# A weight ring of four places instead of five, one more weight pair resident, and the streamed pairs spread anew

## The chip, the core and the metric

The kernel runs on one core of one Trainium2 chip, which it has to itself. The metric is the device time of one execution in microseconds. A kernel's time is the median of several executions. Where one execution was profiled, its own time stands beside the span of its instructions.

## The reference

The reference returns two independent results side by side, `out[0, :, 0:1024]` and `out[0, :, 1024:2048]`, for a sequence of 2048 rows of 1024 channels in bf16.

Part A is a gated long convolution. `k` is run through a causal filter of four taps and multiplied by `v`; the product is convolved along the sequence with `ssm_k` by FFT (length 4096), a skip term with `ssm_D` is added, and all is multiplied by `q`.

Part B is what matters here, a recurrence over 64 segments:

```python
mem = mem0                                   # [1, 8, 1024]
for s in range(64):
    h = concatenate([mem, x[:, 32*s:32*s+32]], axis=1)   # 40 rows
    q, k, v = (einsum('btd,dhe->bhte', h, W) for W in (Wq, Wk, Wv))   # 32 heads of 128
    scores = where(mask, q @ k.T * 128**-0.5, -1e9)
    o = einsum('bhte,hed->btd', softmax(scores) @ v, Wo)
    mem = o[:, :8]                           # goes into the next segment
    outs.append(o[:, 8:])
```

The memory rows of a segment's output are the memory of the next segment, so the 64 steps cannot run side by side. Each step uses the whole of four weight matrices of 1024 x 4096 bf16, 8 MB each and 32 MB together.

## The kernel before

**Stages.** Part A runs first, in three passes, and beside it TensorE already computes what of part B does not depend on the recurrence (the class `Rows`, line 131: the projections of the last eight rows of each segment, kept in DRAM as `QKBd` and `VBd`). Then comes the loop over 64 segments (lines 908 to 991), and last an output product for eight rows of each segment (lines 996 to 1011). All instructions are written out by hand in their order; nothing is scheduled by a planner.

**Weight pairs.** The weights are handled in 64 pairs of 512 KB, tiles `[128, 2, 1024]`, 4 KB in each of the 128 partitions. Key `("qk", g, i)` is input chunk `i` of Wq and Wk for head group `g` (32 pairs); `("v", g, i)` is chunk `i` of Wv for half `g` of the columns (16 pairs); `("o", g, i)` is two heads of Wo (16 pairs). Below, qk26 is short for `("qk", 2, 6)`, and so on. Lines 58 to 63 sort them into three kinds:

- 45 **resident** pairs lie in on-chip memory for the whole loop.
- 2 **parked** pairs, v01 and qk16, lie in PSUM (line 670), and are copied into a ring place each step by ScalarE and VectorE (`unpark`, lines 716 to 720).
- 17 **streamed** pairs are read from DRAM anew in each step, as listed in `STREAM` (line 40), by group: qk02 qk05, qk13, qk22 qk26, qk32 qk36; v00 v03 v05, v11 v15; o02, o11, o20 o23, o32.

**The ring.** Streamed and unparked pairs live in a pool of `RING = 5` places (line 697). `place()` (line 708) takes the next pair of a fixed list `todo` (the streamed pairs in the order of their use, step after step) and issues one DMA of 512 KB on SyncE's queue (line 713). Ahead of the loop it is called `RING` times (line 901). After that it is called by `done(key)` (line 725), right behind the last matmul that read a streamed or unparked pair: the DMA waits for those matmuls, and then fills the place just freed. For two pairs, qk02 and v03, `done` gives the freed place to a parked pair instead (`PARKED`, line 41). So the load of a pair is issued when the use that lies `RING` uses ahead of it has ended, and every place is at each moment loading, holding a pair that waits, being read, or holding an unparked pair.

**A step on TensorE** (lines 918 to 983), with the ring's uses in brackets: group 0's query and key products [qk02, qk05], half of the v products [v00, v01, v03], group 1's [qk13, qk16], the rest of v's first half [v05], group 2's [qk22, qk26], group 3's [qk32, qk36], the second half of v [v11, v15], then the output product `wo` of groups 0 to 3 [o02; o11; o20, o23; o32]. In between stand the transposes (`tr_a`), scores and the products with V (`pv`) of each group, whose softmax runs on VectorE and ScalarE. At the end `Y_sb` (line 985) and `fill_mem` (line 987) put the new memory rows into `hT`, on which the first product of the next step waits.

A pair of the qk or v kind is four matmuls per 512 columns (`qk_part` line 753, `v_part` line 767), one of the o kind eight of 256 columns (`wo` line 874). The matmuls are the same whether the pair is resident, streamed or parked.

**Other traffic of a step**: `qkb` (128 KB, line 794, SyncE's queue), `H` (line 663, ScalarE's queue), `VB`, `OLd` and four small output DMAs (lines 804, 867, 989, GpSimd's queue).

**Around the loop.** Streamed qk and o pairs are first copied into a contiguous layout `Wst` in DRAM (`relay`, line 122); streamed v pairs are read from `Wv` itself. Resident pairs are loaded beside part A (`open_res`, `res_half`), some of the o kind within step 0 (line 911). In the last step the streamed o pairs are loaded once more, into places of resident pairs that are no longer needed (lines 939 to 943), for the final product.

Of the kernel before, what the change touches and what calls it, by code (L numbers as in the profile page):

```python
# [21 lines left out]
def fused_kernel(ctx: ExitStack, tc, q, k, v, shift_k, ssm_k, ssm_D, outa, x, mem0, Wq, Wk, Wv, Wo, outb, n_seg):  # L22
# [13 lines left out]
    NP = 34  # L36
    NS = 17
    scale = 128.0 ** -0.5
    RING = 5
    STREAM = {"qk": ((2, 5), (3,), (2, 6), (2, 6)), "v": ((0, 3, 5), (1, 5)), "o": ((2,), (1,), (0, 3), (2,))}  # L40
    PARKED = {("qk", 0, 2): ("v", 0, 1), ("v", 0, 3): ("qk", 1, 6)}

    msched = tc.manual_schedule()
# [11 lines left out]
    def keys(m, g, r):  # L55
        return [(m, g, i) for i in r]
# [3 lines left out]
    pairs += [key for g in range(4) for key in keys("o", g, range(4))]  # L60
    streamed = [key for key in pairs if key[2] in STREAM[key[0]][key[1]]]
    parked = list(PARKED.values())
# [42 lines left out]
    def open_res(n):  # L105
        if n:
            pool = cw_.enter_context(tc.tile_pool(name=f"b_wres{len(to_open)}", bufs=1))
            if not wide:
                wide["t"] = pool.tile([128, 8, 2, 1024], BF, name="Wearly")
            for _ in range(n):  # L110
                res_pool[to_open.pop(0)] = pool
# [584 lines left out]
    cp.close()  # L696
    ring = cw_.enter_context(tc.tile_pool(name="b_ring", bufs=RING, reuse_waits="tile"))
    open_res(len(to_open))
# [9 lines left out]
    def place():  # L708

        if todo:  # L710
            key = todo.pop(0)
            t = ring.tile([128, 2, 1024], BF, tag="wring", name="wring")
            nc.sync.dma_start(t[:], Wst[key])
            placed.setdefault(key, []).append(t[:])
# [185 lines left out]

    for _ in range(RING):
        place()
# [113 lines left out]
@with_exitstack  # L1016
def kernel(
    ctx: ExitStack,
    tc: tile.TileContext,
    A_q: bass.AP,  # L1020
    A_k: bass.AP,
    A_v: bass.AP,
    A_shift_k: bass.AP,
    A_ssm_k: bass.AP,
    A_ssm_D: bass.AP,
    B_x: bass.AP,
    B_mem0: bass.AP,
    B_Wq: bass.AP,
    B_Wk: bass.AP,
    B_Wv: bass.AP,  # L1030
    B_Wo: bass.AP,
    B_seg_len,
    out: bass.AP,
):
    assert int(B_seg_len) == 32
    S = B_x.shape[1]
    n_seg = S // 32
    outa = out[0, :, 0:1024]
    outb = out[0, :, 1024:2048]
    with ExitStack() as fctx:  # L1040
        fused_kernel(fctx, tc, A_q[0], A_k[0], A_v[0], A_shift_k, A_ssm_k, A_ssm_D, outa, B_x[0], B_mem0[0],
                     B_Wq.rearrange("d h e -> d (h e)"), B_Wk.rearrange("d h e -> d (h e)"),
                     B_Wv.rearrange("d h e -> d (h e)"), B_Wo.rearrange("h e d -> (h e) d"),
                     outb, n_seg)
# [35 lines left out]
```

## Time and profile before

| | us |
|---|---|
| three executions | 2148.29, 2157.45, 2145.75 |
| median | 2148.29 |
| the profiled execution, its own time | 2154.46 |
| its span, first to last instruction | 2152.6 |
| TensorE, matmul busy | 1720.4 (80% of the span) |
| VectorE busy | 1117.8 (52%) |
| ScalarE busy | 921.1 (43%) |
| GpSimd busy | 419.9 (20%) |
| DMA: bytes moved, mean rate | 728.63 MB, 338 GB/s |
| ring loads: number, size | 1083, 512 KB each |

The profile is one execution. Its page gives busy times of the engines, the chain of work that ended last, and the costliest groups of instructions, one line each: line of the kernel, engine, operation, out<-in by the program's names, number, busy time in us, mean ns of one, and the idle time of the engine just ahead of them with what ended it. A TensorE that waits shows as idle time ahead of a group, put down to what released it; a DMA's time is that from its issue to its landing. The span exceeds the sum of the loop's steps by part A ahead of it and the final product behind it: the step-ending copy of line 894 runs 63 times, from 454.8 to 2059.2 us.

### The profile page before, as it was taken

Reading aid. Unit: us, or ns where it says so; the run is one execution under the profiler, and the core shown is the slowest. Engines: PE = TensorE matmul, PEld = TensorE weight load, DVE = VectorE, ACT = ScalarE, POOL = GpSimd, SP = SyncE. Lnnn points to the kernel's source line nnn. Section 1 sums busy time; section 2 is a strip of 40 time slices with the busy share of each in tenths; the row PEclk is TensorE's granted clock in tenths of the full one; section 3 lists DMA queues with packets and bytes.
Section 4 is the critical chain, followed back from the end, with each engine's and each line's share of the span. In section 5 each row is a group of like instructions: output and inputs, shape, how many; then the busy total and the mean of one; then the engine's idle time right before and its main releaser. Section 6 shows DMA issues by size and latency. Waiting matters only on the chain. (4 is left out here: it accounts for less than half of the span.)

```text
span 2152.6 us, 74044 instructions
## 1 busy us (share of the span) xinstructions
PE 1720.4 (80%) x30514; PEld 895.9 (42%) x30514; DVE 1117.8 (52%) x3364; ACT 921.1 (43%) x2282; POOL 419.9 (20%) x1023
## 2 busy tenths in 40 slices
PE   4788987777887887788788888888888878788879
PEld 2332232334443444444444444444444444444448
DVE  6895842245554555555455555555555545555530
ACT  4546741134444444444444444444444444444430
POOL 4003630011111111111111221111111111221110
PEclk8999999889999999999999999999999999999999
DMA  7798969699999999999999999999999999999990
GB/s 238 287 337 312 360 236 355 215 364 360 364 374 323 363 372 368 354 354 352 337 368 369 373 352 372 369 364 365 361 354 367 363 346 375 366 369 371 367 321 22
DMA packets 267375, 728.63 MB, mean 338 GB/s; under 512 B 64751, under 2 KB 75903, under 8 KB 266525
## 3 DMA queue, kind: packets, MB, share of 16 engines
q1 hardware_dynamic: 241294, 687.24, 86.9%
q0 software_dynamic: 15520, 22.06, 3.3%
q10 hardware_dynamic: 10224, 14.62, 1.9%
q8 instruction: 239, 3.92, 0.7%
q14 instruction: 98, 0.80, 0.1%
HBM read 673.52 MB, written 56.56 MB: 339 GB/s over the span
## 5 line engine op out<-in xcount | busy, mean ns | idle before, releaser
L753 PE MATMUL qkacc<-Wqk,hT 128*32 128x512 bf16 x4096 | 339.5, 384 | 0.0
L753 PEld LDWEIGHTS <-hT 128*32 128x32 bf16 x8192 | 185.9, 96 | 241.9 <-issue 92.1
L874 PEld LDWEIGHTS <-OT 128*32 128x32 bf16 x8192 | 210.2, 96 | 108.9 <-issue 59.2
L874 PE MATMUL yacc<-Wo,OT 128*32 128x256 bf16 x5632 | 237.1, 274 | 16.7 <-ACT OT L863 14.7
L753 PE MATMUL qkacc<-wring,hT 128*32 128x512 bf16 x2048 | 207.5, 394 | 32.8 <-DMA wring<-Wstqk 26.5
L767 PE MATMUL vacc<-wring,hT 128*32 128x512 bf16 x1536 | 143.0, 387 | 100.2 <-DMA wring<-in_B_Wv_dram 98.4
L720 DVE COPY wring<-park 128x1024 bf16<-128x1024 bf16 x128 | 88.6, 692 | 242.3 <-PE vacc L767 164.0
L767 PE MATMUL vacc<-Wv,hT 128*32 128x512 bf16 x2560 | 209.8, 382 | 0.0
L767 PEld LDWEIGHTS <-hT 128*32 128x32 bf16 x4096 | 111.3, 95 | 226.4 <-issue 152.4
L833 ACT ACTIVATE P<-S 128x128 bf16<-128x128 f32 x256 | 71.1, 278 | 314.0 <-DVE S L825 233.5
L789 ACT COPY QK<-tp 128x256 bf16<-128x256 bf16 x256 | 95.4, 373 | 237.2 <-PE tp L780 237.2
L788 POOL COPY QK<-qkb 128x64 bf16<-128x64 bf16 x256 | 61.4, 240 | 652.9 <-PE tp L780 487.3
L753 PE MATMUL qkacc<-Wearly,hT 128*32 128x512 bf16 x2048 | 166.4, 403 | 18.5 <-DVE hT L894 17.9
L852 DVE COPY PB<-P 32x160 bf16<-32x160 bf16 x896 | 173.7, 194 | 10.6
L837 DVE TENSOR_REDUCE sm<-P 128x4 f32<-128x256 bf16 x256 | 107.5, 420 | 130.3 <-ACT P L834 130.3
L719 ACT COPY wring<-park 128x1024 bf16<-128x1024 bf16 x128 | 130.7, 1021 | 103.8 <-PE qkacc L753 100.8
L759 ACT CAST qks<-qkacc 128x512 bf16<-128x512 f32 x256 | 150.8, 589 | 28.8 <-PE qkacc L753 23.3
L874 PE MATMUL yacc<-wring,OT 128*32 128x256 bf16 x2520 | 126.4, 274 | 36.2 <-DMA wring<-Wsto 35.2
L863 ACT CAST OT<-otacc 128x256 bf16<-128x256 f32 x256 | 98.4, 384 | 126.8 <-PE otacc L859 126.8
L989 POOL DMA_DIRECT2D out_dram<-Y_sb x256 | 129.1, 511 | 89.9 <-ACT Y_sb L985 87.9
L824 DVE TENSOR_REDUCE mx<-S 128x4 f32<-128x160 f32 x256 | 83.2, 325 | 107.3 <-PE S L821 102.4
L780 PE MATMUL tp<-ident,qks 128*128 128x128 bf16 x1024 | 102.1, 222 | 42.6 <-ACT qks L759 39.3
(216 smaller groups left out, 2827.1 us busy)
## 6 DMA issues: line engine op xcount, KB each, us to landing
wring<-Wstqk SPq DMA_DIRECT2D x448, 512.0 KB, 6.3
wring<-in_B_Wv_dram SPq DMA_DIRECT2D x320, 512.0 KB, 6.7
wring<-Wsto SPq DMA_DIRECT2D x315, 512.0 KB, 6.0
SK<-s_sb SPq DMA_DIRECT2D x8, 1024.0 KB, 7.0
SU<-s_sb SPq DMA_DIRECT2D x8, 1024.0 KB, 6.7
QKBd<-stq ACTq DMA_DIRECT2D x4, 2048.0 KB, 10.9
Kg<-SK SPq DMA_DIRECT2D x16, 512.0 KB, 6.9
Ug<-SU SPq DMA_DIRECT2D x16, 512.0 KB, 7.5
```

The source lines that it names most:

```text
L719: nc.scalar.copy(t[:, 0, :], park[key][0][:])
L720: nc.vector.tensor_copy(t[:, 1, :], park[key][1][:])
L753: nc.tensor.matmul(u.qk[p0:p0 + 32, :], lhsT=hT[:, kc, :], rhs=w[:, t, c2 * 512:(c2 + 1) * 512], start=(kc == 0), stop=(kc == 7), tile_pos ...
L759: nc.scalar.copy(u.qks[:], u.qk[:])
L767: nc.tensor.matmul(vacc[0][32 * c:32 * c + 32, :].rearrange("p (n x) -> p n x", n=2), lhsT=hT[:, kc, :], rhs=w[:, :, c * 256:(c + 1) * 256 ...
L780: nc.tensor.transpose(tp[:, j * 128:(j + 1) * 128], src[:, j * 128:(j + 1) * 128], ident[:])
L789: nc.scalar.copy(u.QT.rearrange("e (c j) r -> e c j r", c=2), tv[:, 0])
L837: nc.vector.tensor_reduce(out=sm[:], in_=Pv.rearrange("p b x k -> p x b k"), op=ALU.add, axis=AX.XY)
L852: (nc.vector if by[c] == "D" else nc.gpsimd).tensor_copy(to, src)
L863: nc.scalar.copy(u.OT[:].rearrange("e (c i) q -> e i c q", i=2), ov[:, :, :, 0:32])
L874: nc.tensor.matmul(Y[32 * dq:32 * dq + 32, 0:256], lhsT=u.OT[:, hh, 0:32], rhs=w[:, hh % 2, dq * 256:(dq + 1) * 256], start=(u.g == 0 and ...
L989: nc.gpsimd.dma_start(outb[32 * s:32 * s + 24, dq * 256:(dq + 1) * 256], Y_sb[32 * dq + 8:32 * dq + 32, :])
```

## The change

Two constants change; no other line does.

```diff
-    RING = 5
-    STREAM = {"qk": ((2, 5), (3,), (2, 6), (2, 6)), "v": ((0, 3, 5), (1, 5)), "o": ((2,), (1,), (0, 3), (2,))}
+    RING = 4
+    STREAM = {"qk": ((2, 5), (3,), (1, 4, 6), (2, 6)), "v": ((3, 5), (1, 5)), "o": ((2,), (1,), (1,), (2,))}
     PARKED = {("qk", 0, 2): ("v", 0, 1), ("v", 0, 3): ("qk", 1, 6)}
```

The ring has four places of 4 KB per partition instead of five, and the memory of the fifth holds a 46th resident pair. The streamed pairs are 16 instead of 17: v00, qk22, o20 and o23 become resident, and qk21, qk24 and o21, resident before, are streamed. In order of use a step's ring uses are now qk02, qk05, [v01], v03, qk13, [qk16], v05, qk21, qk24, qk26, qk32, qk36, v11, v15, o02, o11, o21, o32, the bracketed ones unparked. The order of the work on TensorE, ScalarE and VectorE stays as it was.

## The prediction

> **What bounds the kernel now.** I read first the share of the DMA engines by stretch, then TensorE's waits, then the times from issue to landing, then the timeline of a step.
>
> The DMA engines' busy tenths in 40 slices, from the page, then one stretch of 400 us (columns: busy us of each engine, granted clock, DMA share, GB/s):
>
> ```profile
> DMA  7798969699999999999999999999999999999990
> ```
>
> ```profile
> 1000.00:1400.00 400.00, 323.12 (x6724) 170.42 (x6723) 205.26 (x701) 175.12 (x476) 77.31 (x219) 0.99 0.98 363
> ```
>
> In the loop the DMA engines are busy 98% of the time, TensorE (first number) 81%. The clock is full, so nothing is lost there.
>
> The copy that ends a step, from the instructions of line 894, and TensorE's waits (us in total, times, longest):
>
> ```profile
> L894 DVE COPY hT<-mt_tp x63: 191/192/193, 454.8 to 2059.2; 128x64 bf16<-128x64 bf16 x63
> ```
>
> ```profile
> PE vacc L767 <- DMA wring<-in_B_Wv_dram: 98.4, 151, 8.6
> ...
> PE yacc L874 <- DMA wring<-Wsto: 35.2, 71, 1.3
> ...
> PE qkacc L753 <- DMA wring<-Wstqk: 26.5, 40, 3.4
> ```
>
> (2059.2 - 454.8) / 62 = **25.88 us a step**. TensorE waits for ring loads 98.4 + 35.2 + 26.5 = 160 us, 2.5 us a step. Without them a step takes 25.88 - 2.5 = 23.4; I use 23.5, because a little of ScalarE's work now hides in those waits. Of this floor 21.1 us is matmuls; the rest is the chains through softmax and the new memory rows, and nothing in the change touches them.
>
> The ring loads, from the DMA list and the ring tile's summary (number, size, median us to landing):
>
> ```profile
> wring<-Wstqk SPq DMA_DIRECT2D x448, 512.0 KB, 6.3
> wring<-in_B_Wv_dram SPq DMA_DIRECT2D x320, 512.0 KB, 6.7
> wring<-Wsto SPq DMA_DIRECT2D x315, 512.0 KB, 6.0
> ```
>
> ```profile
> DMA to landing us min/median/max: 3.2/6.3/9.6
> ```
>
> A load takes 6.35 us on the mean, yet 3.24 us when alone (issued at 394.30, with nothing else under way). The difference is queueing. Going through steps 8 to 57, two landings lie 1.44 us apart; only v05's comes 2.07 and o32's 2.41 after the one ahead, because small transfers (VB and outputs; qkb and H) pass between. The sum is 17 x 1.44 + 0.55 + 0.95 = 25.98, which is the step. So **the step is the DMA engines' time**, and the ring is deep enough to keep them full. It also closes over the places: 17 loads x (6.35 loading + 0.48 waiting landed + 0.5 being read and reissued) + 4.8 for the two unparked pairs = 129.4 = 5 places x 25.9.
>
> **The change, part by part.**
>
> *16 loads instead of 17.* That removes 1.44 us of DMA time a step: 16 x 1.44 + 1.5 = 24.54. SyncE issues 63 DMAs fewer (0.33 us each, its time not on the path). The matmuls are as many and of the same shape.
>
> *Four places.* A load is issued when the use four ahead of it has ended, not five. What the lost place costs depends on the time between those two uses. I took each use's mean start from the trace and removed the waits for loads (us from the step's start): qk02 0.55, qk05 1.31, v01 2.42, v03 3.03, qk13 4.45, qk16 5.43, v05 6.21, [qk21 7.69, qk24 8.63,] qk26 9.06, qk32 11.04, qk36 12.14, v11 13.32, v15 15.55, o02 16.64, o11 18.40, [o21 19.30,] o32 21.86. The bracketed uses are new; I place them from the neighbours, 0.21 us a pair. From a use to the one that it frees the place for:
>
> - before (five on): qk05 to v05 4.90, v00 to qk22 5.70, all others over 6.5;
> - after (four on): **qk16 to qk26 3.63, qk13 to qk24 4.18**, qk21 to qk36 4.45, qk24 to v11 4.69, v05 to qk32 4.83, qk05 to v05 4.90, all others over 5.2.
>
> Such a stretch must hold 0.40 of reading, 0.10 to the issue, the load, and 0.04 to the matmul. The heavy place is group 2, where three streamed pairs now lie in 1.4 us and two of the four places have just held unparked pairs.
>
> *Walk through a step.* Issue = end of the freeing use + 0.10. Landing = the later of issue + L and the last landing + 1.44 (+ 0.55 for v05, + 0.95 for o32). A use starts at landing + 0.04 or in its turn, and a wait shifts all behind it. With five places this gives 25.98 for every L up to 5, against 25.88 measured. With four and L = 4.5: v05 is issued at 1.81, lands at 6.31, wait 0.10. qk24 is issued at 4.95, behind qk13, and lands at 9.45 where its turn is 8.73: wait 0.72. qk26 is issued at 5.97, lands 1.44 behind qk24 at 10.89: wait 1.01. qk16 and v11 wait 0.10 together. Sum 1.93; 23.5 + 1.93 = **25.43**. The waits at v00 and v03 are gone, and group 2 is late in their place; its transposes, scores and softmax stand behind qk26 and shift with it, as TensorE's order has nothing to put ahead of them.
>
> *L, a load's time with little ahead of it*, decides. Rows: 3.24 alone; 15 loads that found under one load's packets not yet started: 3.3 to 6.0, median 4.77; loads with three others under way median 6.0, with four 6.5, but those are queueing and belong to the 1.44. By the walk the step is 24.54 for L up to 3.6 (the DMA bound again), 24.93 at 4.0, 25.43 at 4.5, 25.73 at 4.8, 26.03 at 5.0, 27.03 at 5.5. I take 4.5: nearer to 4.77, since in the loop other traffic runs beside, but under it, since ten of the 15 were v pairs, which meet the most small transfers.
>
> The Trainium skill, "DMA: Bandwidth & Descriptors", section "Anatomy of one DMA", gives a fixed 2.0 us plus bytes at 436 GB/s: an estimate of 3.2 us for 512 KB. The lone load (3.24) agrees; by that rule four places would do, and the step would be 24.54. The same page's section "Latency and other measured facts" speaks against the change: memory latency is 0.2 us on average but 2 us at high load, and the fixed part lightens only with the load. Added to 3.2 that is an estimate of 5.0 us, and the step would be 26.03; the 4.77 of the trace lies between the two.
>
> *The rest.* v00 is loaded into resident memory and not the prologue's small ring, the relays are 12 as before, and step 0 loads one resident o pair more and one streamed pair less: nothing, hidden beside part A, with 3 us either way. The last step reloads four o pairs instead of five, ahead of a transfer on which the final product waits (17 us, in the chain): -1.4.
>
> *Sum.* (25.4 - 25.88) x 63 = -30, and -1.4: -32 on the profiled execution's 2154.5, so 2122. That execution lay 6.2 above the median of 2148.3; in terms of the median **2116 us**.
>
> **The rivals.**
>
> 1. *The saving comes in full.* L stays under 3.6, and the step falls to the DMA bound: (24.54 - 25.88) x 63 - 1.4 = -86, median 2062. For it speaks the 3.24; against it that no loaded stretch shows loads this short but for one of the 15.
> 2. *The ring becomes the bound, and the kernel is slower.* One mechanism: the load for qk24 and qk26, issued behind qk13 and qk16, is not shorter than 5.0 because group 2's three loads, VB and the outputs share the engines there. From L = 4.95 the walk passes 25.9. At 5.5 it is 27.03: +1.15 x 63 - 1.4 = +71, median 2219. For it speak the loaded rows (v05's own median is 5.6) and that over the places 4 x 25.9 leaves only 5.7 us a load for loading and waiting, where now 6.8 are spent; against it that most of the 6.35 is queueing, of which one place less removes up to 1.44.
> 3. *Loss and saving cancel*, L near 4.9, within 0.5% (about what a measurement of this kernel can tell from no change, 11 us).
>
> That the change does not do what it says is no case: the built program has 16 ring loads a step on SyncE's queue.
>
> **How the numbers follow.** Chances: my forecast (step 24.9 to 25.7, median 2085 to 2136) 0.42, full saving 0.18, cancelling 0.13, slower 0.27. So faster 0.60, same 0.13, slower 0.27. The likeliest case gives 2116. The 8 in 10 range cuts a tail of each side: 2055, just under the full saving, to 2195, a step of 26.6, which L = 5.3 gives. The forecast's own range is 2085 to 2136.
>
> **What would show it.** Right: 1020 ring loads; a median to landing near 5.1; TensorE's waits for vacc down by more than half, and waits of qkacc for the ring, at qk24 and qk26, of some 1.7 us a step as the longest of its DMA waits; DMA share a little lower, 0.95 or so; the step-ending copies 25.4 apart. Rival 1 would show 0.98 and 24.5, with waits spread over all pairs; rival 2 landings over 5.3 and waits for Wstqk over 2 us a step. Wrong at the root: a step under 24.5, or waits that do not stand in group 2.

## The result and the profile after

| | before | after |
|---|---|---|
| median of 4 executions, us | 2147.02 | 2235.54 |
| lowest to highest | 2139.11 to 2157.45 | 2227.37 to 2238.7 |
| ratio, 95% interval | | 1.0412 (1.0379 to 1.0445) |
| profiled execution: own time / span | 2154.46 / 2152.6 | 2236.32 / 2234.5 |
| a step of the loop | 25.88 | 27.27 |

The kernel is 4.1% slower, where 1.5% faster was predicted; the time lies above the range of 2055 to 2195. (A fourth execution of before came with this result.) An execution over 1.5% above the fastest of its kernel is left out of the ratios given here and below, in experiment 1 three of four.

Of the 81.9 us by which the span grew, the loop has (2141.7 - 450.7) - (2059.2 - 454.8) = 86.6; the part ahead of it became 4.1 shorter and the tail 0.6.

The step, from the instructions of line 894 after: (2141.7 - 450.7) / 62 = 27.27.

```profile
L894 DVE COPY hT<-mt_tp x63: 190/192/193, 450.7 to 2141.7; 128x64 bf16<-128x64 bf16 x63
```

The DMA engines after, from the page and from the same stretch of 400 us (TensorE's busy us first; at the end of the line granted clock, DMA share, GB/s):

```profile
DMA  7799887899998999999999999999999999999990
```

```profile
1000.00:1400.00 400.00, 311.49 (x6496) 165.88 (x6492) 202.18 (x689) 170.69 (x463) 70.43 (x206) 0.99 0.95 329
```

The tenths look as before, and the share fell only from 0.98 to 0.95. But the engines moved 329 GB/s instead of 363, 9% less. The share alone would hide that.

TensorE's waits for ring loads after (us in total, times, longest):

```profile
PE vacc L767 <- DMA wring<-in_B_Wv_dram: 117.4, 103, 7.4
PE qkacc L753 <- DMA wring<-Wstqk: 101.7, 149, 3.0
PE yacc L874 <- DMA wring<-Wsto: 59.0, 98, 1.8
```

They sum to 278 us, 4.4 a step, against 160 and 2.5. The growth of 1.9 is more than the step's 1.39; the rest was given back where other waits became shorter behind a TensorE that comes later (the transposes' wait for `qks` fell from 39.3 us to 12.9). All three kinds of pair wait longer, the q and k pairs by far the most: nearly four times as long.

The loads after, from the DMA list (median us to landing) and the ring tile's summary:

```profile
wring<-Wstqk SPq DMA_DIRECT2D x512, 512.0 KB, 5.8
wring<-in_B_Wv_dram SPq DMA_DIRECT2D x256, 512.0 KB, 5.7
wring<-Wsto SPq DMA_DIRECT2D x252, 512.0 KB, 5.9
```

```profile
DMA to landing us min/median/max: 3.5/5.8/10.7
```

This is the line that decides. The median went from 6.3 to 5.8, not to the 5.1 that the prediction gave as a sign of being right.

Group 2 of one step after, from the timeline (start, duration; in brackets the idle time ahead and its releaser). The four uses are v05, qk21, qk24 and qk26:

```profile
1166.44 0.40 PE L767 MATMUL vacc<-wring,hT 128*32 128x512 bf16 x4 [1.00 <-DMA wring<-in_B_Wv_dram]
...
1167.90 0.40 PE L753 MATMUL qkacc<-wring,hT 128*32 128x512 bf16 x4
...
1169.17 0.40 PE L753 MATMUL qkacc<-wring,hT 128*32 128x512 bf16 x4 [0.27 <-DMA wring<-Wstqk]
...
1170.58 0.40 PE L753 MATMUL qkacc<-wring,hT 128*32 128x512 bf16 x4 [0.79 <-DMA wring<-Wstqk]
```

v05 comes late, and the three pairs behind it start 1.3 to 1.5 us apart; on the mean of steps 8 to 57 their loads land 1.57, 1.53 and 1.37 us after the load ahead, near the 1.44 of a full queue. On the mean of steps 8 to 59 the waits are v05 1.20, qk21 0.10, qk24 0.49, qk26 0.71, then v11 0.34, o02 0.23, o21 0.49, o32 0.17, and under 0.15 each elsewhere.

### The profile page after: what moved, and what is told of

Same layout as the page of the kernel before. It is cut to its first block, busy times and chain, and to the rows that moved or that the text cites. A ratio compares the mean times of both kernels' runs of the same rounds, so it can differ in the third digit from the quotient of the medians.

```text
span 2234.5 us, 73957 instructions
## 1 busy us (share of the span) xinstructions
PE 1741.9 (78%) x30485; PEld 907.6 (41%) x30514; DVE 1123.8 (50%) x3364; ACT 928.6 (42%) x2282; POOL 416.9 (19%) x1023
## 5 line engine op out<-in xcount | busy, mean ns | idle before, releaser
L753 PEld LDWEIGHTS <-hT 128*32 128x32 bf16 x8192 | 190.5, 97 | 332.1 <-issue 191.4
L753 PE MATMUL qkacc<-wring,hT 128*32 128x512 bf16 x2304 | 238.0, 401 | 108.6 <-DMA wring<-Wstqk 101.7
L874 PE MATMUL yacc<-Wo,OT 128*32 128x256 bf16 x6144 | 251.4, 274 | 18.2 <-ACT OT L863 17.0
L767 PE MATMUL vacc<-Wv,hT 128*32 128x512 bf16 x2816 | 238.6, 388 | 0.0
L767 PE MATMUL vacc<-wring,hT 128*32 128x512 bf16 x1280 | 129.4, 390 | 119.6 <-DMA wring<-in_B_Wv_dram 117.4
L767 PEld LDWEIGHTS <-hT 128*32 128x32 bf16 x4096 | 112.3, 96 | 228.0 <-issue 146.8
L865 DVE CAST OL<-otacc 128x64 bf16<-128x64 f32 x252 | 52.4, 208 | 209.2 <-ACT OT L863 208.5
L874 PE MATMUL yacc<-wring,OT 128*32 128x256 bf16 x2016 | 100.9, 275 | 61.0 <-DMA wring<-Wsto 59.0
```

The lines of the kernel that those rows point to most:

```text
L753: nc.tensor.matmul(u.qk[p0:p0 + 32, :], lhsT=hT[:, kc, :], rhs=w[:, t, c2 * 512:(c2 + 1) * 512], start=(kc == 0), stop=(kc == 7), tile_pos ...
L767: nc.tensor.matmul(vacc[0][32 * c:32 * c + 32, :].rearrange("p (n x) -> p n x", n=2), lhsT=hT[:, kc, :], rhs=w[:, :, c * 256:(c + 1) * 256 ...
L874: nc.tensor.matmul(Y[32 * dq:32 * dq + 32, 0:256], lhsT=u.OT[:, hh, 0:32], rhs=w[:, hh % 2, dq * 256:(dq + 1) * 256], start=(u.g == 0 and ...
```

## The experiments

Two theories were put against each other. **A**: four places are too few for 512 KB loads, because a load hardly gets shorter when one fewer is under way; the new spread is not to blame. **B**: the new spread, with three streamed pairs in group 2, is to blame. Later ones look at why v05 is late although little lies ahead of it. A step is always that between the copies that end a step (line 894, in some kernels a few lines off) in the profiled execution, and a load's time the mean from issue to landing in the loop. The traces tell the landing of 86 to 88% of the loads, and the means are over these.

**1. Before, with four places** (17 loads, the old spread).

```diff
-    RING = 5
+    RING = 4
```

> Four places alone, with the old 17 streamed pairs in their old spread. Theory A (a ring load with little ahead of it takes some 5.4 us in the loop, not 4.5, and the stretch from a use to the fourth after it is too short for that): the walk through a step gives 29.6 us a step at 5.35 us a load, so 2148 + 3.7 x 63 = about 2380 us; at 4.5 us a load it would be 27.0 and 2220. Rival B (the new spread is at fault, three streamed pairs crowded into group 2): the old spread has no such crowd, so the time stays within 30 us of before, under 2180.

Measured: 2429.45 us, the median of four executions between 2388.8 and 2437.2. The profiled one took 2426.7 us at a granted clock of 0.925, the shortest 2388.8 at 0.944. Its step is 30.30 and its load 5.72, against 6.39 with five places. Waits stand at v03 0.74, qk13 1.14, v05 0.84 and o23 1.58: at other pairs than after, since the old spread has other short windows. A part of the 30.30 can be TensorE's lower clock. The shortest execution lies 243 us above before (2145.3), so one place costs some 3.9 us a step by itself, near the 3.7 of A's walk, and B falls.

**2. After, with five places** (16 loads, the new spread). Memory has no room for it, so pair o33 is left out and its products read o31.

```diff
-    RING = 4
+    RING = 5
...
+        key = ("o", 3, 1) if key == ("o", 3, 3) else key
```

> Sixteen loads alone: the new spread with five places. There is no memory for it, so the pair o33 is neither loaded nor kept, and its matmuls read o31 instead (as many matmuls of the same shape). Theory A: the stretches are five uses long again, the walk gives 24.8 us a step at 5.35 us a load, so about 2148 - 66 = 2082 us, DMA busy 0.97 or more. Rival B: group 2 still has its three streamed pairs, TensorE still waits there over 1 us a step, and the time is not under 2140.

Measured: 2061.97 us, ratio 0.9614 (0.9557 to 0.9672); step 24.67, load 6.23. The prediction's bound for 16 loads was 24.54. The stretch and the landings of this kernel:

```profile
1000.00:1400.00 400.00, 335.10 (x7172) 180.72 (x7172) 221.83 (x761) 187.78 (x511) 79.03 (x228) 0.99 0.99 360
```

```profile
DMA to landing us min/median/max: 3.3/6.3/10.6
```

The DMA engines are full again. TensorE's waits for v pairs, which cost 117.4 us after, have almost gone:

```profile
PE qkacc L754 <- DMA wring<-Wstqk: 76.8, 105, 5.1
...
PE vacc L768 <- DMA wring<-in_B_Wv_dram: 17.9, 19, 4.3
PE yacc L875 <- DMA wring<-Wsto: 5.4, 17, 0.9
```

So the streamed pairs of the change are worth what was forecast, and the place costs 27.27 - 24.67 = 2.60 us a step, twice what the load saves (25.88 - 24.67 = 1.21). In the old spread, too, the place costs more than a load saves (experiment 1), so the place is the loss in both.

**3. Before, with four places and one o load fewer** (16 loads in the old windows).

```diff
-    RING = 5
-    ... "o": ((2,), (1,), (0, 3), (2,))}
+    RING = 4
+    ... "o": ((2,), (1,), (0,), (2,))}
```

> Four places and 16 loads as in the changed kernel, but in the old spread with only o23 made resident. Theory A: the tight stretches are now qk05 to qk13 (3.14 us) and v00 to v05 (4.01 us), the walk gives 28.3 us a step at 5.35 us a load, so about 2300 us, slower than the changed kernel, with the waits at qk13 and v05. Rival B (the new spread is at fault): not above 2160.

Measured: 2286.52 us, ratio 1.0649 (1.0580 to 1.0717); step 28.12. A's walk had 28.3. The new spread is 0.85 us a step better than this one, so against the old windows it is a gain, not the loss.

**4. After, without small transfers**: the output stores of all steps but the last, and the VB reloads, are left out.

```diff
-            nc.gpsimd.dma_start(outb[...], Y_sb[...])
-        if not last:
-            load_vb(s + 1)
+            if last:
+                nc.gpsimd.dma_start(outb[...], Y_sb[...])
```

> The changed kernel without the small output stores of line 989 (but for the last step's) and without the reloads of VB after the first; output rows and the products with VB are then not the reference's. Theory A in its general form (any load with little ahead takes 5.4 us): v05 still takes over 5 us, the step stays at about 26.7 to 27.2, the time above 2200 us. Rival C (loads are long because those small transfers run beside them at the start of a step): v05's load falls to 4.5 us or less, the step to about 25.4, the time to 2120 us.

Measured: 2225.53 us, ratio to before 1.0369 (1.0300 to 1.0438), which overlaps that of after; step 26.93, v05's load 5.0 instead of 5.36. The small transfers have about 0.35 us of v05's load and not the main part.

**5. After, with three places.**

```diff
-    RING = 4
+    RING = 3
```

> The changed kernel with three places (the memory of the fourth unused). At most three loads are under way, so little queueing is left and the landing times show what a load takes by itself. Theory A (a floor of 5.0 to 5.4 us in the loop, whatever is under way): median to landing 5.0 or more, the walk gives 33 to 36 us a step, the time 2600 to 2760 us. Rival F (the 5.4 of four places is still queueing, and a load falls towards the lone 3.24 as fewer are under way): median 4 us or less, the step under 29, the time under 2350 us.

Measured: 2615.7 us in one execution, beside 2150.7 for before; step 33.23, load 4.98.

```profile
1000.00:1400.00 400.00, 279.58 (x5227) 142.06 (x5221) 161.45 (x550) 137.62 (x372) 57.75 (x168) 0.91 0.81 264
```

```profile
DMA to landing us min/median/max: 3.1/5.0/9.2
```

The means of qk13 (4.28) and qk21 (4.23) are the lowest here, but they mix two kinds of load. Of the 38 landings of qk13 in steps 8 to 57, 14 took 3.14 to 3.39 us and 23 took 4.63 to 5.39. What tells them apart is the backlog. A load is 128 packets of 4 KB, so one can count how many packets of earlier ring loads have yet to start when a load is issued (steps 1 to 62; median us from issue to landing, and number of loads):

| packets yet to start | 0 | 1 to 63 | 64 to 127 | 128 to 255 |
|---|---|---|---|---|
| three places | 3.21 (17) | 4.47 (138) | 4.88 (310) | 5.27 (403) |
| four places, 17 loads (experiment 1) | 3.27 (15) | 4.48 (42) | 4.94 (121) | 5.78 (628) |

The 14 short loads of qk13 had 0 to 3 packets ahead of them, the 23 long ones 13 to 66. So the 3.24 of the lone load is reached inside the loop, by loads with almost nothing of the ring ahead, and less than half a load ahead already costs over 1 us. Why the step between the two is so large is not shown. The sentence in the expectation of experiment 9 on qk13 and qk21, "a load that found nothing ahead took 4.2 to 4.3 us", does not hold.

**6. After, with the streamed v pairs laid out contiguously too**, like the q, k and o pairs; so far their 4 KB rows are read 8 KB apart from `Wv`.

```diff
-    relaid = [key for key in streamed if key[0] != "v"]
+    relaid = list(streamed)
...
-    for m, g, i in streamed:
-        if m == "v":
-            Wst[m, g, i] = Wv[...]
```

> The changed kernel, with the streamed v pairs also copied once into the contiguous layout ahead of the loop, as the qk and o pairs are, and streamed from there. Rival E (v05 and v15 are long because their 4 KB rows lie 8 KB apart in Wv): their loads fall below 4.8 and 5.4 us, the step by 0.6 us, the time to 2200 us or less. Theory A (any load with little ahead): as the changed kernel, 2225 to 2245 us.

Measured: 2212.84 us, ratio to before 1.0261 (1.0182 to 1.0340), an interval that lies below that of after; step 27.04. v05's load fell from 5.36 to 4.52 and the mean of its packets from 248 to 194 ns (v15's from 217 to 181). The layout is part of v05's lateness, but the step gains only 0.23 of the 0.84 (0.36 by the medians): the time falls between the two expectations. The 8 KB alone cannot be the reason: v03, whose rows lie in the same way, went from 176 to 169 ns only, and in experiment 2 v05's packets took 178 ns without the copy. The copy changes the spacing of the rows and their place in DRAM, and no run parts the two.

**7. After, each ring load as two DMAs of 256 KB.**

```diff
-        nc.sync.dma_start(t[:], Wst[key])
+        for n in range(2):
+            nc.sync.dma_start(t[:, n, :], Wst[key][:, n, :])
```

> The changed kernel, each ring load issued as two DMAs of 256 KB (2 KB a row). Theory A with a floor that is per DMA and not per byte: the halves land as late as the whole, the second 0.3 us later for its issue, the time 2230 to 2280 us. Rival D (the long part of a load is its own bytes on its slowest engine): the halves land in 4.5 us or less and the time falls under 2190 us.

Measured: 2350.8 us in one execution; step 29.07. Half the bytes take 5.1 us at the median, the whole took 5.8:

```profile
DMA to landing us min/median/max: 2.6/5.1/8.6
```

The halves queue beside each other: from the first half's issue to the second's landing 5.83 us pass on the mean, as for the whole load of after. Smaller pieces in the same four places are worse, by more than A had expected, and rival D's fall did not come. Their rows are 2 KB; such packets took 97 ns on the mean, twice 97 against 185 for one of 4 KB. Why the step grew by 1.8 us with a pair landing as soon, this run does not show.

**8. Four places, with the 16 loads spread by the walk of the prediction** (fed with 5.4 us a load).

```diff
-    STREAM = {"qk": ((2, 5), (3,), (1, 4, 6), (2, 6)), "v": ((3, 5), (1, 5)), "o": ((2,), (1,), (1,), (2,))}
+    STREAM = {"qk": ((2, 5), (2,), (3, 4, 7), (2,)), "v": ((3, 6), (0, 2, 6)), "o": ((2,), (0,), (3,), (0,))}
```

> Four places and 16 loads with a spread chosen by the walk at 5.4 us a load among those that the order of the prologue's loads allows: qk02 qk05 v03 qk12 v06 qk23 qk24 qk27 qk32 v10 v12 v16 o02 o10 o23 o30. Theory A: the walk gives 26.2 against 26.8 for the changed kernel, so 40 us faster than it, about 2195 us, and still slower than before (2148). Rival B (another spread would bring the gain of the 16 loads, 2065 to 2090): under 2140 us.

Measured: 2265.82 us, ratio 1.0532 (1.0487 to 1.0576); step 27.72. This expectation failed, the time even has the other sign against after. The walk behind it had left out the small transfers that pass ahead of v06 (0.55 us) and o30 (0.95). With them, reckoned after the run, it gives 27.03 for this spread and 26.83 for the changed one: slower, as measured, but by 0.2 where 0.45 was found. Waits stand at qk24 1.08, qk27 0.68 and o30 1.10. Only three spreads were run with four places, so a better one is not excluded.

**9. After, with two places.**

```diff
-    RING = 4
+    RING = 2
```

> The changed kernel with two places, so that a load finds at most one other under way. With three places a load that found nothing ahead took 4.2 to 4.3 us (qk13, qk21) and one behind another 5.2. Theory A as it stands now (some 4.2 us from issue to landing with nothing ahead, more with a load ahead): median to landing 4.2 to 4.7, the walk gives 42 to 46 us a step, the time 3150 to 3400 us. Rival F (a load alone takes 3.24 as the one lone load of the profile did, all above is queueing): median under 3.7, the step under 38, the time under 2900 us. A floor of 5.0 whatever is ahead would give 48 us and 3540.

Measured: 3278.85 us in one execution, beside 2147.9 for before; step 43.66, load 4.26.

```profile
1000.00:1400.00 400.00, 252.67 (x4034) 121.42 (x4033) 125.81 (x426) 108.95 (x288) 43.03 (x130) 0.80 0.66 203
```

With three of five places gone, a load still takes two thirds of its time with five. Both a floor of 5.0 and rival F fall. A part of the longer step can be TensorE's clock, 0.80 in this stretch.

**10. Experiments 4 and 6 together** (it leaves out the same stores and reloads as 4).

> The changed kernel with both edits that shortened v05's load: the contiguous copy of the streamed v pairs, and no small output stores nor reloads of VB (output rows and the products with VB are then not the reference's). If v05's load alone made the loss, it falls to 4.2 us, and the step to 25.4, about 2120 us. If the loads of the whole step are too long for four places (theory A), the two edits add up to what each gave, 22 and 10 us: 2195 to 2210 us, with loads of 5.0 to 5.5 us elsewhere.

Measured: 2206.29 us, ratio 1.0260 (1.0216 to 1.0305); step 26.55. v05's load is 4.26, all others lie between 4.9 and 6.4. With v05 under the 4.5 us that the prediction took, the kernel is still 2.6% slower than before, and the step (of the shortest execution, 2191.3 us) is 26.55 where the prediction had 25.43: v05 alone is not the loss. v05, qk24 and qk26 wait 0.23, 0.74 and 1.08, close to the forecast for group 2 (0.10, 0.72, 1.01); the rest of the loss stands at other pairs.

**11. Before, with the contiguous v pairs** (five places, 17 loads; the edit of 6).

> The kernel before, five places and 17 loads, with the streamed v pairs copied once into the contiguous layout ahead of the loop. If rows 8 KB apart cost the DMA engines time also where the queue is deep: v05's packets took 210 ns on the mean there against 164 to 179 for the others, so 0.1 to 0.2 us a step, 6 to 12 us faster, 2136 to 2142. If a deep queue hides it (theory A): no change that can be measured, 2140 to 2156; the four more copies ahead of the loop may cost 3 us.

Measured: 2123.98 us over six executions, ratio 0.9895 (0.9863 to 0.9928); step 25.41. It is 1.1% faster than before, by more than the gain that was expected, with all of the work done. v05's load fell from 5.62 to 5.16, its packets from 210 to 184 ns, v15's from 179 to 164.

```profile
1000.00:1400.00 400.00, 328.29 (x6852) 173.78 (x6845) 208.50 (x714) 178.15 (x484) 77.07 (x220) 0.98 0.99 367
```

It moves 367 GB/s instead of 363, at a DMA share of 0.99. But v00 and v03, read in the same way before, kept their packets (165 to 164 and 164 to 162 ns), so here too the copy helped v05 and v15 and not all rows 8 KB apart.

**12. After, with six places** (o30 and o33 are left out, their products read o31).

```diff
-    RING = 4
+    RING = 6
...
+        key = ("o", 3, 1) if key in (("o", 3, 3), ("o", 3, 0)) else key
```

> The new spread of 16 loads with six places; two pairs have no memory and are left out (the matmuls of o30 and o33 read o31 instead, as many and of the same shape). Two, three, four and five places gave steps of 43.7, 33.2, 27.3 and 24.7 us, with 1.6, 2.4, 3.4 and about 4 loads under way, each load taking some 0.8 us longer per load more under way. Theory A with the DMA engines full at 24.5 us a step: no more to gain, loads of 7 us or more, 2045 to 2065 us. If the engines still had room at five places (a load's time keeps rising by only 0.8 us per load under way): the step falls to the floor of 23.5 to 23.9, about 2000 us.

Measured: 2068.25 us, ratio 0.9650 (0.9580 to 0.9720); step 24.70, load 6.71. The sixth place brings nothing over the fifth; the load grows instead. (Theory A had expected 7 us or more, and 2045 to 2065 us.)

```profile
DMA to landing us min/median/max: 3.1/7.0/9.7
```

The granted clock of this execution was 0.958, against 0.968 with five places. The shortest executions, 2053.6 us (clock 0.967) and 2057.1 (0.974), leave room for a small gain only. It is also no longer the ring that TensorE waits for:

```profile
PE x_tp L886 <- DMA H<-in_B_x_dram: 79.8, 62, 2.7
...
PE qkacc L754 <- DMA wring<-Wstqk: 9.7, 11, 2.7
```

The waits for ring loads, 100.1 us with five places, have almost gone, and TensorE waits instead for `H`, the 64 KB of the next segment's rows: 79.8 us, against 40.9 with five places and 11.3 before. `H` lands 6.1 us after its issue at the median, against 5.3 and 4.8. From two places to six, with 16 loads, its median is 3.6, 4.3, 5.1, 5.3 and 6.1: a deeper ring makes this small transfer late. So the floor of 23.5 is not reached either where the ring's waits are gone: `H` has 79.8 / 63 = 1.3 us of the 24.70.

**The runs side by side.** Loads under way are loads a step x load time / step. Packets are DMA packets of 4 KB, nearly all of the ring, of which the median is 159 ns in every one. Where 16 loads have five or six places, pairs are left out as in experiments 2 and 12.

| places, loads | step | load | under way | mean packet ns | DMA share, GB/s |
|---|---|---|---|---|---|
| 2, 16 | 43.66 | 4.26 | 1.56 | 208 | 0.66, 203 |
| 3, 16 | 33.23 | 4.98 | 2.40 | 197 | 0.81, 264 |
| 4, 16 (after) | 27.27 | 5.75 | 3.37 | 185 | 0.95, 329 |
| 5, 16 | 24.67 | 6.23 | 4.04 | 175 | 0.99, 360 |
| 6, 16 | 24.70 | 6.71 | 4.35 | 175 | 0.97, 354 |
| 5, 17 (before) | 25.88 | 6.39 | 4.20 | 174 | 0.98, 363 |

From two places to four, a load grows by (5.75 - 4.26) / (3.37 - 1.56) = 0.8 us for each load more under way.

## Why the prediction was wrong, point by point

**Right: what bounds the kernel before, and what a load less is worth.** 24.54 was forecast for 16 loads with a ring deep enough; the run with five places has 24.67. (Of the small transfers, v05's is 2.07 - 1.44 = 0.63 by the prediction's own spacings, not 0.55.) For the tail -1.4 was forecast and -0.6 measured; the part ahead of the loop, put within 3 us, changed by -4.1. The 1020 ring loads and the share of 0.95 are as foreseen.

**Right: the form of the walk and the second rival.** It named the mechanism, a ring that becomes the bound, from a load time of 4.95 on, and priced it at 27.03 and 2219 us for a load of 5.5; measured are 27.27 and 2235.5. Fed with 5.35, the walk gives 26.73 and starts v05 at 7.20, qk24 at 10.34 and qk26 at 11.78, where the trace has 7.31, 10.51 and 11.87. The sum over the places comes to 16 x (5.75 + 0.36 waiting landed + 0.5) + 4.8 = 110.6, which over four places is 27.6; it is an account of the places' time and closes whatever the bound is. Of this rival's two signs the landings over 5.3 came; the waits for `Wstqk` were 101.7 / 63 = 1.6 us a step, under the 2 that it gave.

**Wrong: L, the term that decides.** The step that failed reads "I take 4.5", and ahead of it the dismissal of the rows with more under way: "those are queueing and belong to the 1.44". In the changed kernel v05's load took 5.36, and the 118 loads of steps 1 to 62 that found under one load's packets of the ring not yet started took 5.12 at the median.

Part of this was a reading. Counted as in experiment 5, the trace of before has 33 loads with under 128 packets ahead in steps 1 to 62, and their median is 5.35; a median of 4.77 comes out only for the 13 with under 100. And the difference between 6.35 and 3.24 was taken for a queue that one place less shortens by up to a whole 1.44. The runs show a third to a half of it: a place less takes 0.48 us off a load (16 loads) or 0.67 (17 loads, at the lower clock of experiment 1). The break-even stood in the prediction itself: loading and waiting landed had to fall from 6.83 to (4 x 25.9 - 4.8) / 16 - 0.5 = 5.68, by 1.15, and fell to 5.75 + 0.36 = 6.11, by 0.72. The rows of 6.0 with three others under way and 6.5 with four had said so, 0.5 for each, and three others are what four places allow.

**Wrong as well: the landing behind another load.** L accounts for 26.73 - 25.43 = 1.30 us of the 1.84 by which the step came out above the forecast. The walk lets a load that has others ahead land 1.44 us after the last of them. v11, v15, o02 and o21 landed 1.69 to 1.81 us after it on the mean of steps 8 to 57, though they had been issued 3.7 to 4.4 us before that landing. Experiment 10 shows the same from the other side: with v05's load at 4.26 the walk would give no more than 25.43, and the step is 26.55.

**Wrong: where TensorE waits.** v05 was put at 0.10 and has 1.20. Only 49 packets of earlier ring loads, under half a load, have yet to start at its issue on the mean. Its window is 4.9 us, and its load takes 5.36. The contiguous copy takes 0.84 off this load (experiment 6), leaving out the small transfers 0.35 (experiment 4), both 1.10 (experiment 10). The window of 4.9 is the same before, and so is a long load (5.62); but there the waits at v00 and v03, 0.40 and 0.58 us a step, stretched the window, and the change took these waits away.

qk24 and qk26 were put at 1.73 and have 1.20. In after and experiments 4, 6 and 10 these two wait 1.20, 1.51, 1.67 and 1.82 while v05 waits 1.20, 0.74, 0.44 and 0.23: what v05 does not wait, they wait in part. The waits at v11, o02, o21 and o32, 1.23 together, were all but absent from the forecast (v11 had a part of 0.10); their windows, from 4.69 (v11) over 5.60 (o02) and 5.98 (o21) to 6.31 (o32), must hold loads of 5.5 to 6.1 and 0.54 besides. So the promise "waits for vacc down by more than half" failed (98.4 to 117.4).

**The two estimates of a load's time.** The lone load's 3.24 us agreed with the estimate of 3.2 from the Trainium skill, "DMA: Bandwidth & Descriptors", section "Anatomy of one DMA", although that section fits it to DMAs issued from GpSimd and these are issued from SyncE. In the loop it held for loads with nothing of the ring ahead (3.21 and 3.27 in the table of experiment 5) but not for v03 and v05 with two places (4.06 and 3.88), nor with a larger backlog; for 256 KB, where it would give an estimate of 2.6, the shortest took 2.6 and the median was 5.1. The estimate of 5.0 from the Trainium skill, "DMA: Bandwidth & Descriptors", section "Latency and other measured facts", was the nearer to the 5.75 of after, but by luck: that section counts the memory's latency as the main part of the fixed 2.0 us, so that adding it to 3.2 counts it twice. The Trainium skill, "Perfetto Trace Analysis", section "Identifying the Most-Contended Engine", says to judge DMA by the bandwidth used and not by occupancy, since 16 engines make occupancy misleading; the last column of the table agrees.

**Open.** Why packets grow longer on the mean when fewer loads are under way, no run here tells. With two places v03 and v05, with nothing of the ring ahead, took 4.06 and 3.88 us at the median, where qk13 and, in experiment 8, v06 took 3.2 to 3.3; why is not shown either. Of the 0.47 us a step that the contiguous layout gained with five places (0.38 by the medians), the shorter packets of v05 and v15 account for about 0.33, eight of each on each of the 16 engines; other pairs' packets changed both ways (qk26 from 167 to 184 ns), and the rest is not explained.

## What to carry to other kernels

A ring's step is the sum of what each load holds a place, over the number of places; before taking a place away, take the load time from the rows with that many loads under way, and ask whether it falls by as much as the lost place demands. Here load and wait together fell by 0.7 us where 1.15 was needed. A DMA share near 1 bounds what fewer bytes can bring, but it does not say that the depth that fills it can be spared, and the layout of the rows that are streamed (1.1% here, by experiment 11) is worth a look before either. A load's time read at a small backlog should come with the backlog that was counted: here it ran from 3.2 us with nothing ahead to 5.8 with one to two loads ahead.

## What the runs showed of the hardware

- About four loads of 512 KB under way on the mean went with 360 GB/s; 3.4 with 329, 2.4 with 264, 1.6 with 203.
- A load with none of the ring's packets ahead took 3.2 to 3.3 us in the loop (three places, and experiment 1), as alone, though v03 and v05 took 4.06 and 3.88 with two places; with up to half a load ahead 4.5, with one to two loads ahead 5.3 and 5.8.
- With fewer loads under way the mean packet became longer (174 to 208 ns, the median staying at 159): 1.9% of the ring's packets took over 400 ns with five places, 8.0% with two. So the busy share falls more slowly than the rate: 0.95 for 329 GB/s, where 329 of the 363 at 0.98 would be 0.89.
- v05's packets, rows of 4 KB read 8 KB apart, took 248 ns in the changed kernel and 194 when laid out contiguously; v03's, read in the same way, 176 and 169.
- TensorE's granted clock in the stretch was 0.99 with four and five places, 0.91 with three, 0.80 with two, where it was busy 280 and 253 of 400 us instead of 311 and 335. With six places it was busy 334 us at a clock of 0.95, so idle time alone does not give the clock.
